# Sixteen experts on one Trainium2 core: smaller rooms by rank, unsplit first layers for seven experts, short last blocks in four column groups

## The chip, the cores and the metric

The kernel runs on one core of a Trainium2 chip. The metric is device microseconds for one execution of the whole program, and the lower number is the better one. Each kernel is one launch; its time is the median of several runs, and beside them stands one execution that the hardware profiler recorded.

## What is computed

Two stages follow one another. The first is a recurrent attention over 4 batches x 8 heads x 768 steps x 40 channels. The second routes its 3072 rows of 320 numbers to 16 experts (4 groups of 4), one expert for each row, and each expert is a two-layer network with 1024 hidden units. The second stage is the one that the change touches:

```python
g_idx = np.argmax(x @ w_group, axis=1)
for g in range(G):
    xg = x[g_idx == g]
    e_idx = np.argmax(xg @ w_expert[g], axis=1)
    for e in range(Eg):
        h = np.maximum(xg[e_idx == e] @ w1[g, e], 0.0)     # 320 -> 1024
        ye = h @ w2[g, e]                                  # 1024 -> 320
        out[tok_idx] = combined[:, None] * ye              # weights of both softmaxes
```

Everything is fp32.

## The kernel before

**Rooms.** The experts are handled one after another in the order of their token counts, the fullest first. The program is fixed before the counts are known, so the expert of rank `r` gets a room of `CAPS[r]` token slots, and all tiles and instructions of rank `r` have that size. With the inputs of this case the reference routes 321, 290, 274, 257, 242, 239, 209, 193, 165, 158, 139, 135, 132, 126, 125 and 67 tokens to the experts by rank. Tokens over a room are left to a loop at the end (`For_i` over `total`, L1048), which takes blocks of 128 tokens, fetches index, rows and both weights anew for each, and runs zero times when every room is large enough. Rank 0 is handled in two parts, `EARLY` and `LATE`.

**One expert** is one call of `expert()`. Its rows `xg` are gathered from DRAM by GpSimd in blocks of 128 (L564), turned on TensorE (`tpm`, three transposes a block) and copied to `xhl`. The first layer makes the hidden units in eight groups `f` of 128 (tile `psh`, three buffers), the ReLU brings them to `hh` (ScalarE the high part L683, VectorE the low part L686; `hh` has one buffer), and the second layer (tile `po`, two buffers) multiplies them with the second weights, a block of up to 128 tokens at a time; the result goes through ScalarE into `y` (L762) and is scattered to the output (L568).

**Precision.** TensorE takes fp32 in two passes, so most operands are split into a high and a low part of a type that takes one pass, and the products that matter are added up. The weights arrive as fp32 in `w1s` (1.5 MB) and `w2s` (1.3 MB), each with two buffers, sent by SyncE's queue; ScalarE rounds them to `w1h`, `w2h` (L624) and VectorE subtracts to get `w1l`, `w2l` (L626). There are three kinds of first layer. A split one has 8 matmuls of W columns for each `f` (L729, 64 rows for an expert, where W is the room). A side-by-side one (`NARROW`) has high and low tokens side by side, two matmuls of W and three of 2W columns for each `f` (40 rows). An unsplit one (`FULL`) has 3 fp32 matmuls for each `f` (L697), each shown as two passes (48 rows), and needs no split of `w1s`. In the second layer a full block has three matmuls for each `f` (L750 to L752, 24 rows). A last block of at most 64 tokens, here called a half block, has its high and low tokens side by side and needs two (L755 and L756, 16 rows); its two halves are then added up by VectorE (L764 to L766).

**Order.** The loop `for r in range(NEARLY, NE)` first issues the loads for rank r+2 (`load_ix`, `load_w1`, `load_w2`, `load_x`) and puts the split of the next expert's weights (`split_tasks(r + 1)`) among the ReLUs of rank r: three pieces of `w1s` before the first layer, the four pieces of `w2s` one behind each ReLU. The turns of rank r+1 follow the first layer of rank r (`then`). SyncE and GpSimd each work through their DMAs in order, so a transfer that waits holds back the ones behind it.

## Time and profile before

| what | value |
|---|---|
| median of 3 runs | 445.42 us |
| lowest and highest of them | 444.24 and 445.44 us |
| the profiled execution | 445.48 us |
| its span, first to last instruction | 443.8 us |
| around the span | 1.7 us |
| TensorE busy, share of the span | 398.2 us, 90% |
| VectorE, ScalarE, GpSimd busy | 280.1, 220.4 and 176.3 us |
| mean granted TensorE clock | 0.881 |
| expert stage | about 190 to 438 us |

The page cuts the span into 40 slices of 11.1 us; a digit is the busy share of a slice in tenths. A second view used below takes stretches of time and gives each engine's busy time in them, for one tile alone: a stretch from an expert's first matmul of a kind to its last is the length of that stage.

### The profile page before, as it was taken

How to read it: one execution, taken by the hardware profiler on the slowest of the kernel's cores; microseconds unless marked ns; L12 is line 12 of the kernel's file. 1: busy time of each engine (PE TensorE's matmuls, PEld its weight loads, DVE VectorE, ACT ScalarE, POOL GpSimd, SP SyncE). 2: the span in 40 equal slices, each digit the busy share in tenths (PEclk: the TensorE clock that was granted, in tenths of full speed). 3: DMA queues.
4: the chain of work that ended last, by engine and by line, in shares of the span. 5: the costliest groups of instructions: out<-in, count | busy, mean ns of one | idle time of the engine just before them, and what ended most of it. 6: DMA issues, size and time to landing. Idle time of an engine off the chain costs nothing.

```text
span 443.8 us, 13468 instructions
## 1 busy us (share of the span) xinstructions
PE 398.2 (90%) x5470; PEld 357.5 (81%) x5470; DVE 280.1 (63%) x712; ACT 220.4 (50%) x570; POOL 176.3 (40%) x213
## 2 busy tenths in 40 slices
PE   6688796887787799699999999999999999999994
PEld 2376565765565588499999999999999999999994
DVE  5466285786656875774964665857675878767420
ACT  1426242634445360533854565756474766766421
POOL 4256355555455724545314134333214516322210
PEclk9659685989788755579999999999999999999998
DMA  8826457788795865248966457576676667544400
GB/s 212 228 78 203 145 150 208 213 236 259 221 273 168 250 187 201 60 97 316 371 226 222 150 202 246 199 266 220 203 285 241 212 202 299 194 146 140 158 16 9
DMA packets 29730, 87.80 MB, mean 198 GB/s; under 512 B 11537, under 2 KB 15577, under 8 KB 26051
## 3 DMA queue, kind: packets, MB, share of 16 engines
q1 hardware_dynamic: 24292, 69.52, 49.4%
q0 software_dynamic: 5152, 16.93, 11.1%
q8 instruction: 43, 0.70, 0.7%
q10 hardware_dynamic: 224, 0.49, 0.4%
q14 instruction: 19, 0.16, 0.1%
HBM read 76.77 MB, written 11.01 MB: 198 GB/s over the span
## 4 chain that ended last, share of the span: by engine, by line
PE 69%; issue 10%; DVE 7%; DMA 5%; POOL 4%; ACT 3%; POOLq 1%; SPq 0%; ACTq 0%
PE psh L729 20%; PE po L750 6%; PE po L751 6%; PE po L752 6%; PE busy L134 4%; PE X L254 4%; PE tpm L291 2%; ACT ab L175 2%; PE X L190 2%; PE po L756 2%; PE po L755 2%; PE tp L291 2%; DMA nt<-in_nat_dram 2%; PE psh L697 1%; PE Y L230 1%
## 5 line engine op out<-in xcount | busy, mean ns | idle before, releaser
L175 ACT ACTIVATE ab<-aw,bcol 128x64 f32<-128x64 f32 x192 | 41.9, 332 | 64.0 <-PE aw L172 62.1
L564 POOL DMA_INDIRECT xg<-x_d,ix x34 | 40.2, 1183 | 81.1 <-PE po L752 29.1
L568 POOL DMA_INDIRECT out_dram<-y,ix x34 | 39.8, 1171 | 78.5 <-ACT y L762 64.5
L750 PE MATMUL po<-w2h,hh 128*128 128x320 f32 (+1 forms) x208 | 65.7, 316 | 0.0
L751 PE MATMUL po<-w2l,hh 128*128 128x320 f32 (+1 forms) x208 | 64.2, 309 | 0.0
L752 PE MATMUL po<-w2h,hh 128*128 128x320 f32 (+1 forms) x208 | 64.2, 309 | 0.0
L626 DVE TENSOR_TENSOR w2l<-w2s,w2h 128x640 fp32r<-128x640 f32 x64 | 50.6, 822 | 20.2 <-ACT w2h L624 20.1
L729 PE MATMUL psh<-xhl,w1h 128*128 128x256 f32 (+4 forms) x352 | 60.3, 293 | 2.6 <-DVE xhl L669 2.0
L729 PEld LDWEIGHTS psh<-xhl,w1h 128*128 128x128 f32 x352 | 51.1, 195 | 3.1 <-DVE xhl L669 2.3
L683 ACT ACTIVATE hh<-psh 128x512 fp32r<-128x512 f32 (+5 forms) x68 | 33.4, 491 | 33.7 <-PE psh L729 24.9
L686 DVE SCALAR_TENSOR_TENSOR hh<-psh,hh 128x256 fp32r<-128x256 f32 (+2 forms) x104 | 39.5, 411 | 16.8 <-ACT hh L683 16.2
L624 ACT CAST w2h<-w2s 128x640 fp32r<-128x640 f32 x64 | 43.1, 728 | 0.0
L750 PEld LDWEIGHTS po<-w2h,hh 128*128 128x128 f32 (+1 forms) x208 | 38.9, 187 | 0.1
L751 PEld LDWEIGHTS po<-w2l,hh 128*128 128x128 f32 (+1 forms) x208 | 38.9, 187 | 0.0
L752 PEld LDWEIGHTS po<-w2h,hh 128*128 128x128 f32 (+1 forms) x208 | 38.8, 187 | 0.0
L626 DVE TENSOR_TENSOR w1l<-w1s,w1h 128x1024 fp32r<-128x1024 f32 x26 | 31.7, 1219 | 11.1 <-ACT w1h L624 7.6
L729 PE MATMUL psh<-xhl,wsk 128*128 128x256 f32 (+4 forms) x176 | 36.9, 292 | 0.0
L729 PE MATMUL psh<-xhl,w1l 128*128 128x256 f32 (+4 forms) x176 | 36.8, 291 | 0.0
L134 PE MATMUL busy<-ones_b 128*128 128x512 bf16 x85 | 34.5, 539 | 2.2 <-DVE sep L900 1.2
L762 ACT ACTIVATE y<-po,xg 128x320 f32<-128x320 f32 (+1 forms) x26 | 13.7, 529 | 45.4 <-PE po L752 43.2
L471 POOL DMA_INDIRECT itab<-tokid,slot x24 | 26.7, 1111 | 22.8 <-DVE slot L402 10.3
L285 POOL TENSOR_TENSOR x<-xn,den 128x320 f32<-128x320 f32 x20 | 15.8, 789 | 45.8 <-DVE xn L280 42.6
(198 smaller groups left out, 866.8 us busy)
## 6 DMA issues: line engine op xcount, KB each, us to landing
w1s<-in_w_dram SPq DMA_DIRECT2D x12, 1536.0 KB, 7.4
w2s<-in_w_dram SPq DMA_DIRECT2D x12, 1280.0 KB, 6.7
nt<-in_nat_dram SPq DMA_DIRECT2D x24, 488.0 KB, 4.6
qk<-in_qkT_dram SPq DMA_DIRECT2D x24, 448.0 KB, 6.2
x_d<-x SPq DMA_DIRECT2D x24, 192.0 KB, 3.0
w1s<-in_w_dram SPq DMA_DIRECT2D x8, 384.0 KB, 4.8
w1s<-in_w_dram POOLq DMA_DIRECT2D x2, 1536.0 KB, 7.5
w2s<-in_w_dram SPq DMA_DIRECT2D x8, 320.0 KB, 5.0
```

Source lines behind the costliest of these rows:

```text
L134: mm(t, ones_b, bc(ones_b.unsqueeze(1), (P, 4, P)), start=True, stop=True)
L175: rt["exp"] = nc.scalar.activation(ab[:, i, :], aw[:, i, :], AF.Exp, bias=bcol[:, u, i:i + 1])
L564: return nc.gpsimd.indirect_dma_start(out=o, out_offset=None, in_=src, in_offset=bass.IndirectOffsetOnAxis(ap=idx, axis=0))
L568: return nc.gpsimd.indirect_dma_start(out=out, out_offset=bass.IndirectOffsetOnAxis(ap=idx, axis=0), in_=y, in_offset=None, bounds_check=N ...
L624: nc.scalar.copy(a, src[:, s])
L626: lows.append(lambda: nc.vector.tensor_tensor(o[rows], src[rows, s], a[rows].bitcast(F32), op=ALU.subtract))
L683: act = nc.scalar.activation(hr, src, AF.Relu)
L686: nc.vector.scalar_tensor_tensor(hh[:, f:f + per, dst], src[:, :, t], 0.0, hr.bitcast(F32)[:, :, t], op0=ALU.max, op1=ALU.subtract)
L729: ins = mm(ps[:, g * W:(g + 1) * W], w[:, s], x, start=(n == 0), stop=(n == len(todo) - 1))
L750: mm(po[0:m], hh[:, f, t], w2h[:, s], start=st0, stop=False)
L751: mm(po[0:m], hh[:, f, t], w2l[:, s], start=False, stop=False)
L752: ins = mm(po[0:m], hh[:, f, tl], w2h[:, s], start=False, stop=sp0)
```

## The change

The rooms are smaller: rank 1 goes from 352 to 304, ranks 2 and 3 from 320 and 288 to 288 and 272, and so on to rank 15 from 128 to 96; the second part of rank 0 goes from 128 to 80. Seven experts (ranks 9 to 15) have unsplit first layers instead of three, and ranks 7 and 8 instead of 11 and 12 have side-by-side ones. In `TAIL` are ranks 2, 3, 9, 10, 11 and 12, whose last block has 32 or 16 tokens. It is computed by a new function `short()`: the low part of its hidden units is not made, the fp32 ReLU `h32` is multiplied with the raw `w2s` in 8 fp32 matmuls (two passes each), and these go in turn to four groups of 32 columns of the array, which write four groups of 32 partitions of `po`. ScalarE copies the first group, VectorE adds the other three and multiplies. For three-block experts the short block is issued before block 1, for two-block ones at the end. Because the short block reads `w2s`, a `TAIL` expert issues `load_w2(r + 2)` behind that block's matmuls (`freed`) instead of at the top of the loop, and the new unsplit experts issue `load_w1(r + 2)` behind their first layer, as the old ones did. A half block may now be narrower than the 64 columns that it uses; GpSimd zeroes the rest.

```diff
--- before.py
+++ after.py
@@ -45,16 +45,19 @@
 
 
 
-NEARLY, NPICK, EARLY, LATE = 1, 2, 256, 128
-CAPS = [EARLY + LATE, 352, 320, 288, 256, 256, 256, 256, 192, 192, 192, 192, 160, 160, 160, 128]
-
-
-NARROW = ((0, 1), (11, 0), (12, 0))
+NEARLY, NPICK, EARLY, LATE = 1, 2, 256, 80
+CAPS = [EARLY + LATE, 304, 288, 272, 256, 240, 224, 208, 176, 160, 144, 144, 144, 128, 128, 96]
+
+
+NARROW = ((0, 1), (7, 0), (8, 0))
 
 RETIRE = ((2, 0), (5, 0), (8, 0), (11, 0), (13, 0), (14, 0))
 
 
-FULL = (13, 14, 15)
+FULL = tuple(range(9, NE))
+
+
+TAIL = tuple(r for r in range(1, NE) if 0 < CAPS[r] % P <= 32)
 
 
 def bc(ap, shape):
@@ -670,18 +673,30 @@
 
         return [lambda i=i, m=m: one(i, m) for i, m in enumerate(blocks(W))]
 
-    def expert(key, W, ws, xg, idx, between=(), then=None, last=None):
+    def expert(key, W, ws, xg, idx, between=(), then=None, last=None, freed=None):
         xhl = xhls[key]
         w1h, w1l, wsk, w2h, w2l = (ws.get(n) for n in ("w1h", "w1l", "wsk", "w2h", "w2l"))
 
         nf = W // P * P if 0 < W % P <= 64 else W
         mp = W - nf
-        hh = pools["hp"].tile([P, NF, 2 * W], F32R, name="hh")
+        tail = key[0] in TAIL
+        mq = 0 if tail else -(-mp // 32) * 32
+        hh = pools["hp"].tile([P, NF, 2 * (nf + mq)], F32R, name="hh")
+        if mq > mp:
+            for a in (W, W + mq):
+                nc.gpsimd.memset(hh[:, :, a:a + mq - mp].bitcast(F32), 0.0)
+        if tail:
+            h32 = pools["hp"].tile([P, NF, mp], F32, name="h32")
 
         def relu(f, per, src):
-            hr = hh[:, f:f + per, 0:W]
-            act = nc.scalar.activation(hr, src, AF.Relu)
-            for dst, t in ((slice(W + mp, 2 * W), slice(0, nf)), (slice(W, W + mp), slice(nf, W))):
+            hr = hh[:, f:f + per, 0:nf if tail else W]
+            act = nc.scalar.activation(hr, src[:, :, 0:nf] if tail else src, AF.Relu)
+            if tail:
+                nc.vector.tensor_scalar(h32[:, f:f + per, :], src[:, :, nf:W], 0.0, None, op0=ALU.max)
+                nc.vector.scalar_tensor_tensor(hh[:, f:f + per, nf:2 * nf], src[:, :, 0:nf], 0.0, hr.bitcast(F32),
+                                               op0=ALU.max, op1=ALU.subtract)
+                return act
+            for dst, t in ((slice(nf + 2 * mq, 2 * (nf + mq)), slice(0, nf)), (slice(nf + mq, W + mq), slice(nf, W))):
                 if t.start < t.stop:
                     nc.vector.scalar_tensor_tensor(hh[:, f:f + per, dst], src[:, :, t], 0.0, hr.bitcast(F32)[:, :, t],
                                                    op0=ALU.max, op1=ALU.subtract)
@@ -736,9 +751,26 @@
         if key in NARROW:
             with tc.issue_after(act.ins):
                 do(between)
-        for i, m in enumerate(blocks(W)):
+        def short(i, m):
+            po = pools["ps_o"].tile([P, DM], F32, name="po")
+            for f in range(NF):
+                g = 32 * (f % 4)
+                mm(po[g:g + m], h32[:, f, :], w2st[key[0]][:, f * DM:(f + 1) * DM], start=(f < 4), stop=(f >= 4))
+            if freed:
+                freed()
+            y = pools["hp"].tile([P, DM], F32, name="y", bufs=3)
+            nc.scalar.copy(y[0:m], po[0:m])
+            for g in range(32, P, 32):
+                nc.vector.tensor_tensor(y[0:m], y[0:m], po[g:g + m], op=ALU.add)
+            nc.vector.tensor_scalar(y[0:m], y[0:m], xg[i][0:m, 3 * P:3 * P + 1], None, op0=ALU.mult)
+            no_order("out", scatter(y[0:m], idx(i, m, 1)))
+
+        nb = blocks(W)
+        for i, m in enumerate(nb[:-1] if tail else nb):
+            if tail and i == 1:
+                short(len(nb) - 1, mp)
             t = slice(i * P, i * P + m)
-            tl = slice(W + mp + i * P, W + mp + i * P + m)
+            tl = slice(nf + 2 * mq + i * P, nf + 2 * mq + i * P + m)
             po = pools["ps_o"].tile([P, DM], F32, name="po")
             for f in range(NF):
                 s = slice(f * DM, (f + 1) * DM)
@@ -753,7 +785,7 @@
                 else:
                     if not st0:
                         mm(po[0:m], hh[:, f, t], w2l[:, s], start=False, stop=False)
-                    mm(po[0:2 * m], hh[:, f, nf:nf + 2 * m], w2h[:, s], start=st0, stop=sp0)
+                    mm(po[0:2 * mq], hh[:, f, nf:nf + 2 * mq], w2h[:, s], start=st0, stop=sp0)
                     if st0:
                         mm(po[0:m], hh[:, f, t], w2l[:, s], start=False, stop=False)
             y = pools["hp"].tile([P, DM], F32, name="y", bufs=3)
@@ -761,11 +793,13 @@
             if m > 64:
                 nc.scalar.activation(y[0:m], po[0:m], AF.Copy, scale=comb)
             else:
-                nc.scalar.copy(y[0:m], po[m:2 * m])
+                nc.scalar.copy(y[0:m], po[mq:mq + m])
                 nc.vector.tensor_tensor(y[0:m], y[0:m], po[0:m], op=ALU.add)
                 nc.vector.tensor_scalar(y[0:m], y[0:m], comb, None, op0=ALU.mult)
             done = scatter(y[0:m], idx(i, m, 1))
             no_order("out", done)
+        if tail and len(nb) == 2:
+            short(1, mp)
         if key in RETIRE:
 
             with tc.issue_after(done.ins):
@@ -1029,7 +1063,8 @@
             load_ix(r + 2)
             if r not in FULL:
                 load_w1(r + 2, nc.gpsimd if r < 2 else None)
-            load_w2(r + 2, nc.gpsimd if r < 2 else None)
+            if r not in TAIL:
+                load_w2(r + 2, nc.gpsimd if r < 2 else None)
             xgs[r + 2] = load_x(CAPS[r + 2], ix_of(r + 2))
         if r + 1 < NE:
             split = split_tasks(r + 1)
@@ -1040,7 +1075,8 @@
             then = []
         if r in FULL and r + 2 < NE:
             then.append(lambda r=r: load_w1(r + 2))
-        expert((r, 0), CAPS[r], wsp_[r], xgs[r], ix_of(r), split, then)
+        freed = (lambda r=r: load_w2(r + 2)) if r in TAIL and r + 2 < NE else None
+        expert((r, 0), CAPS[r], wsp_[r], xgs[r], ix_of(r), split, then, freed=freed)
 
 
     hp = pools["hp"]
```

Three places show how the instructions move. First TensorE at the end of rank 9 (`po` and `hh` are its second layer and hidden units) and the start of rank 10 (`psh`), before:

```order
L755 MATMUL po_5696<-w2l_5403,hh_5562 64x320
L756 MATMUL po_5696<-w2h_5402,hh_5562 128x320
L729 MATMUL psh_5743<-xhl_5653,w1h_5553 128x192 x4
L729 MATMUL psh_5743<-xhl_5653,wsk_5555 128x192 x2
L729 MATMUL psh_5743<-xhl_5653,w1l_5554 128x192 x2
L729 MATMUL psh_5743<-xhl_5653,w1h_5553 128x192 x4
L729 MATMUL psh_5743<-xhl_5653,wsk_5555 128x192 x2
```

and of the changed kernel:

```order
L782 MATMUL po_5605<-w2h_5463,hh_5537 128x320
L783 MATMUL po_5605<-w2l_5464,hh_5537 128x320
L784 MATMUL po_5605<-w2h_5463,hh_5537 128x320
L758 MATMUL po_5635<-w2s_5178,h32_5538 32x320 x8
L712 MATMUL psh_5666<-xhl_5589,w1s_5358 128x144 x6
L712 MATMUL psh_5680<-xhl_5589,w1s_5358 128x144 x6
L712 MATMUL psh_5692<-xhl_5589,w1s_5358 128x144 x6
```

The pairs of the half block are gone: a full block of three matmuls for each `f` is followed by eight short ones of 32 rows, and the first layer of rank 10 is unsplit.

Second SyncE's queue from the first weights of rank 11 to those of rank 12, before:

```order
L582 DMA w1s_5545<-in_w1_dram 128x3072 [waits DMAHW0_49,DVE_49]
L582 ISA
L582 DMA w2s_5547<-in_w2_dram 128x2560 [waits DMAHW7_49,DMAHW1_49,DVE_49]
L574 TENSOR_LOAD ewi_69
L597 ISA
L597 DMA ix_5723<-itab_58 128x2x2 [waits DMASW3_49,DMASW4_49,DMASW2_49,DMASW1_49]
L582 ISA
L582 DMA w1s_5725<-in_w1_dram 128x3072 [waits DMAHW3_49,DVE_49]
```

and of the changed kernel:

```order
L585 DMA w1s_5603<-in_w1_dram 128x3072 [waits DMAHW0_49,PE_49]
L585 ISA
L585 DMA w2s_5644<-in_w2_dram 128x2560 [waits DMAHW1_49,DMAHW7_49,DVE_49,PE_49]
L577 TENSOR_LOAD ewi_69
L600 ISA
L600 DMA ix_5658<-itab_58 128x2x2 [waits DMASW3_49,DMASW2_49,DMASW1_49]
L585 ISA
L585 DMA w1s_5730<-in_w1_dram 128x3072 [waits DMAHW3_49,PE_49]
```

Both loads of weights now wait for TensorE (`PE_49`), `w1s` for the first layer of two ranks earlier and `w2s` for the short block of two ranks earlier; the index load `ix` of rank 12 stands behind both.

Third ScalarE from the copy of rank 9's last block on, through the first layer of rank 10, before (`w2h_5763` is the high part of rank 11's second weights):

```order
L764 COPY y_5713<-po_5696 64x320
L624 CAST w2h_5763<-w2s_5547 128x640 x4
L683 ACTIVATE hh_5742<-psh_5743 128x2x192
L683 ACTIVATE hh_5742<-psh_5767 128x2x192
L683 ACTIVATE hh_5742<-psh_5789 128x2x192
L624 CAST w1h_5913<-w1s_5725 128x1024 x2
L683 ACTIVATE hh_5742<-psh_5811 128x2x192
```

and of the changed kernel (`w2h_5676` is the same):

```order
L762 COPY y_5646<-po_5635 32x320
L693 ACTIVATE hh_5664<-psh_5666 128x2x128
L693 ACTIVATE hh_5664<-psh_5680 128x2x128
L693 ACTIVATE hh_5664<-psh_5692 128x2x128
L627 CAST w2h_5676<-w2s_5644 128x640 x3
L693 ACTIVATE hh_5664<-psh_5704 128x2x128
L627 CAST w2h_5676<-w2s_5644 128x640
```

The pieces of rank 11's `w2s` stood ahead of all ReLUs (`hh`) of rank 10 and now stand ahead of the last of the four only; they wait for a load that is issued later.

## Rows read from the trace of the kernel before

**Rows 1.** Page, slices of the span: TensorE's busy tenths and its granted clock.

```profile
PE   6688796887787799699999999999999999999994
...
PEclk9659685989788755579999999999999999999998
```

**Rows 2.** First layers by stretch (`psh`): length, PE, PEld, DVE, ACT busy (count), clock, DMA.

```profile
205.87:211.04 5.17, 5.04 (x40) 4.69 (x40) 1.54 (x6) 1.70 (x7) 1.00 0.77 203
216.17:226.03 9.86, 9.86 (x61) 9.73 (x61) 3.62 (x7) 3.28 (x7) 1.00 0.97 367
237.45:246.99 9.54, 9.54 (x64) 9.29 (x64) 3.72 (x14) 3.06 (x7) 1.00 0.47 159
257.36:265.92 8.56, 8.56 (x64) 8.48 (x64) 3.50 (x14) 2.90 (x7) 1.00 0.50 167
321.52:329.03 7.51, 7.51 (x64) 7.47 (x64) 2.06 (x3) 1.80 (x3) 1.00 0.82 293
336.72:343.85 7.13, 7.13 (x64) 7.12 (x64) 1.76 (x6) 1.47 (x3) 1.00 0.95 345
377.69:384.22 6.53, 6.49 (x40) 5.71 (x40) 1.92 (x6) 2.05 (x7) 1.00 0.65 221
390.73:396.62 5.89, 5.80 (x40) 5.21 (x40) 1.71 (x6) 1.90 (x7) 1.00 0.67 243
403.12:409.64 6.52, 6.52 (x48) 6.44 (x48) 1.66 (x6) 1.31 (x3) 1.00 0.58 214
428.86:434.14 5.28, 5.28 (x48) 5.28 (x48) 1.27 (x3) 1.16 (x3) 1.00 0.10 33
```

**Rows 3.** Second layers by stretch (tile `po`), the same columns.

```profile
226.93:237.45 10.52, 10.52 (x72) 10.39 (x72) 0.00 (x0) 1.06 (x2) 1.00 0.65 224
397.19:400.80 3.61, 3.61 (x25) 3.60 (x26) 0.00 (x0) 0.00 (x0) 1.00 0.19 56
400.80:403.12 2.32, 2.32 (x18) 1.80 (x15) 0.00 (x0) 0.53 (x1) 1.00 0.20 35
```

**Rows 4.** Turns of two blocks (`tpm`), TensorE alone: length, busy (count), clock, DMA.

```profile
396.62:397.19 0.57, 0.57 (x6) 1.00 0.12 29
```

**Rows 5.** Timeline of TensorE in attention: start, length, line, operation, tiles, shapes, count.

```profile
128.61 0.86 PE L336 MATMUL lg<-xT,wc 128*32 128x128 f32 x24
129.40 0.68 PE L254 MATMUL X<-nt,pt 64*64 64x41 f32 x32
```

**Rows 6.** Timeline of VectorE from a half block's evacuation (rank 12) on.

```profile
403.77 0.48 DVE L765 TENSOR_TENSOR y<-y,po 32x320 f32<-32x320 f32 x1 [1.81 <-ACT y L764]
404.28 0.37 DVE L766 TENSOR_SCALAR y<-y,xg 32x320 f32<-32x320 f32 x1
404.58 1.54 DVE L626 TENSOR_TENSOR w2l<-w2s,w2h 128x640 fp32r<-128x640 f32 x2
```

**Rows 7.** Timeline of ScalarE there: the copy, then pieces of `w2h`.

```profile
403.32 0.42 ACT L764 COPY y<-po 32x320 f32<-32x320 f32 x1 [1.80 <-PE po L756]
403.64 1.97 ACT L624 CAST w2h<-w2s 128x640 fp32r<-128x640 f32 x3
```

**Rows 8.** DMA issues from 349 to 425 us: count, KB, median us to landing.

```profile
w2s<-in_w_dram SPq DMA_DIRECT2D x4, 1280.0 KB, 7.4
...
xg<-x_d,ix POOLq DMA_INDIRECT x7, 6.3
```

**Rows 9.** The load of `w2s` issued at 402.0 us, no other running.

```profile
DMA to landing us min/median/max: 5.9/5.9/5.9
```

**Rows 10.** Loads at 349.8 (`w1s`) and 355.0 us (`w2s`): starts, landings of both.

```profile
L582 SPq DMA_DIRECT2D w1s<-in_w_dram x1: 333/333/333, 349.8 to 349.8; - x1
...
L582 SPq DMA_DIRECT2D w2s<-in_w_dram x1: 333/333/333, 355.0 to 355.0; - x1
...
DMA to landing us min/median/max: 7.4/8.1/8.8
```

**Rows 11.** Three gathers of `xg` issued from 348 to 367 us.

```profile
DMA to landing us min/median/max: 8.7/8.7/9.9
```

## The prediction

> **What bounds the kernel now.** I read the slices of the page first [rows 1]. From the nineteenth slice to the last but one TensorE is busy nine tenths or more in every slice and its granted clock is nine tenths or more of full speed; ahead of that, in the attention that the change leaves alone, both vary. The stretches of the expert stage say the same without rounding: in every first layer TensorE's busy time is the length of the stretch to within 0.13 us, in every second layer it is equal to it, and the clock column reads 1.00, the upper of its two levels (2.4 GHz) [rows 2, 3]. So the expert stage is bound by TensorE alone, no wait ends last in it, and each microsecond of TensorE work that goes shortens the span until something else is late. The first question is thus what the removed and added matmuls cost, the second which load or engine no longer keeps up.
>
> **Smaller split first layers.** Now 352, 320, 288, 256 and 192 columns take 10.34 (9.86 for 61 of 64 rows), 9.54, 8.56, 7.51 and 7.13 us [rows 2]. From 320 to 288 that is 0.031 us a column; from 256 to 192 it is nearly flat, and 7.13/64 = 111 ns a row looks like a floor that the weight loads set (PEld is as busy as PE there). Rank 1 (304) lies midway between 9.54 and 8.56, 9.05: -1.29. Rank 2 (288): 8.56 - 9.54 = -0.98. Rank 3 (272) midway between 8.56 and 7.51, 8.03: -0.53. Rank 4 stays at 256. Ranks 5 and 6 (240, 224) go to the floor, 7.13: -0.38 each, -0.76. Sum **-3.6**.
>
> **Side by side.** 192 and 160 columns take 6.53 and 5.89, 0.02 us a column [rows 2]. Rank 7 (208) gives 6.85 for 7.51: -0.66. Rank 8 (176) gives 6.21 for the 7.13 of 192 split columns: -0.92. The late part of rank 0 falls from 128 to 80; no row goes below 128. By 0.02 us a column it would be -0.96, by a floor of 111 ns a row nothing much (5.17/40 is 129 ns already for 128 and 256 columns); I take -0.35 and keep 0 to -1. Sum **-1.9**.
>
> **Unsplit first layers.** 160 columns take 6.52 and 128 take 5.28 [rows 2], so 144 midway 5.90. Rank 9 (160 for 192 split): 6.52 - 7.13 = -0.61. Rank 10 (144 for 192 split): -1.23. Rank 11 (144 for 192 side by side): -0.63. Rank 12 (144 for 160 side by side): 0. Ranks 13 and 14 (128 for 160): -1.24 each. Rank 15 falls from 128 to 96: its row is 110 ns, the floor of the split rows, so I take 0 and keep -1.3 (in proportion to the columns) as the other end. Sum **-4.95**.
>
> **Second layers.** Full blocks are 10.52/3 = 3.51 us, or 3.61 alone, a half block is 2.32 [rows 3]. Rank 1's third block has 48 tokens for 96, so 16 rows for 24: 2.32 - 3.51 = -1.19. Ranks 13 and 14 lose their second block: -2 x 2.32 = -4.64, and its turn, half of 0.57 [rows 4]: -0.57. Sum **-6.4**.
>
> **Short blocks in column groups.** Six half blocks (ranks 2, 3, 9 to 12) become 16 passes of 320 columns, four of them at a time. The unsplit row of 110 ns for 128 columns gives 275 ns for 320. That four groups run at once is seen in attention: 24 fp32 passes of 128 columns, in groups of 32 columns, start at 128.61 and the next matmul starts at 129.40 [rows 5], 0.79 us where 24 x 0.11 = 2.64 would be needed one by one; six sets of 0.11 are 0.66, and 0.13 is entry and exit. So a short block is 4 x 0.275 + 0.13 = 1.23 us against 2.32: -1.09 each, **-6.5**. If they ran one by one it would be 16 x 0.275 = 4.4.
>
> The cuts add up to -23.4 (-3.6, -1.9, -4.95, -6.4, -6.5).
>
> **What the evacuation costs.** A short block is copied in 0.42 [rows 7], then has three additions of 0.48 and one multiplication of 0.37 [rows 6]: 2.2 us, where now 1.3. I put it at nothing, since `po` has two buffers: the next block uses the other one, and the short block's own comes up again 3.6 us later at the earliest. The four ReLUs of the next first layer come one in 1.5 us and find three `psh` buffers, so they can be a microsecond late as well. The zeroing on GpSimd (ranks 1, 8) lies beside a first layer of over 6 us.
>
> **What the later loads cost.** This is the term with a sign against the change. A load of `w2s` took 5.9 us with nothing beside it and 8.8 (the larger of the two landings) when `w1s` had left 5.2 us before it and gathers ran beside it [rows 9 to 11]; the median of four is 7.4 [rows 8]. In ranks 9, 10 and 11 `w2s` of two ranks on leaves at the end E of the short block. In the next rank ScalarE makes three ReLUs, then waits for that load, makes three pieces of `w2h` (1.97 us [rows 7]) and only then the last ReLU, which VectorE follows with 0.56 of its low part behind its own pieces (0.77 each [rows 6]). So that low part is there at X + 3.7, with X the landing after E. TensorE wants it at the third matmul of `f` = 6 of block 0: 5.90 (first layer) + 0.57 (turn) + 20 x 0.147 = 9.4 after E. The stall is X - 5.7. With X = 7.4, the median, which also lies midway between the two ends, it is 1.7 in each of ranks 10, 11 and 12: 5.1. In rank 3 the load of rank 4's `w2s` leaves after rank 2's short block, with `w1s` long ahead of it; the same count along its longer first layer gives X - 5.6, and X of 6.4 near the clear row gives 0.8. For rank 14 the load leaves about 1.4 us ahead of the end of rank 12's short block, and X - 5.0 with 7.4 - 1.4 gives 1.0 in rank 13. Rank 5's load overwrites a buffer that is free early and leaves before rank 3's short block: nothing. Sum **+6.9**. All loads at 5.9 (and 0.1 to issue) give about +1.3; all at 8.8 give 3 x 3.2 + 3.3 + 2.5 = +15.4. Next in line behind these are the gathers, which in the new order of SyncE's queue have their index load behind `w2s`.
>
> **The sum.** 445.5 (the profiled execution, which equals the median of 445.4) - 23.4 + 6.9 = 429.0: I forecast **429 us**.
>
> **Rivals.**
>
> (a) The loads are hidden: TensorE is shifted by so much that they land in time, or nothing runs beside them. Then 445.5 - 23.4 + 1.3 = 423.4, with no stall 422, and 421 if rank 15's first layer follows its columns. For it: ScalarE and VectorE no longer split `w1s` for four more experts (ranks 9 to 12). Against: `w1s` leaves 5.4 us ahead of `w2s` in ranks 9 to 11, as at 355 us [rows 10].
>
> (b) The loads are all late (+15.4, 437.5), or the gathers too: beside weights they took 8.7 to 9.9 us [rows 11], and in ranks 12 to 14 they now leave after an index load that stands behind `w2s`. One to two us for each of three ranks make it 435 to 443.
>
> (c) The evacuation becomes the bound of the short blocks. Its chain is 2.2 us against 1.23 on TensorE; if the next matmuls waited for it in each of six, it would be 6 x 1.0 more: 435. Against it stands the second `po` buffer. The Trainium skill, "TensorEngine Tiling (Array Packing)", section "PSUM Bottleneck", says that tiling speeds up the matmuls and not the copy out of PSUM, which may then be the bottleneck; no row of before shows a block with four groups to add up, and the two engines that it advises to use together are the ones that this chain uses.
>
> (d) The groups don't overlap in fp32 matmuls of 320 columns that accumulate in one bank: 4.4 us for a block in place of 1.23, six times, 19.0 more, 448; with the waits of (a) it would be 442.5, with something between them no change. Against it speak the 24 passes in 0.79 us [rows 5], which have the same type and the same groups of 32 columns.
>
> (e) The slower side: one room is too small. The reference routes 239 tokens to a room of 240 in rank 5, 158 to 160 in rank 9 and 126 to 128 in rank 13; the spare places are 1 to 29, and the count that decides is made in the kernel from its own logits. If a single token is over in any rank the loop at the end runs once, with nothing beside it: an index gather of up to 6.3, rows and weights 7.4 [rows 8], a first layer of 5.28 [rows 2], 16 passes of 0.275, that is 4.4, and a scatter taken to be as long as a gather, some 25 us: 429 + 25 = 454. It decides from the first token over.
>
> **How the numbers follow.** My forecast (424 to 435 around 429) has a chance of 0.72; (a) 0.10; (b) 0.09; (c) 0.02; (d) 0.03; (e) 0.04. The range reaches down to 422, where the cuts come in full, and up to 437, where all loads take 8.8 us; left out are the last part of (a), the upper half of (b), (d) and (e), 0.02 + 0.05 + 0.07 = 0.14. A measurement of this kernel can tell about 0.3% (1.3 us) from no change. Faster by more than that: 0.72 + 0.10 + 0.09 + 0.02 = 0.93; within it, the better part of (d): 0.02; slower, (e) and the rest of (d): 0.05.
>
> **What would show it.** Right: stretches of about 5.9 us for the first layers of ranks 10 to 12 and 5.3 for ranks 13 and 14; a short block of 1.2 us in which sixteen passes start in four sets; TensorE idle some 1 to 2 us in block 0 of ranks 10, 11 and 12, ended by a ReLU whose engine waited for `w2s`; loads of `w2s` near 7.4 us there; the clock still at 1.00. Wrong: passes of the short block that start 0.28 us apart (d); idle TensorE ahead of a turn, ended by a gather (b); idle time after a short block that VectorE's `y` ends (c); a body of the loop at the end (e); no idle time at all (a). The forecast fails by more than its range if a pass of a short block has a cost that the 128-column matmuls of attention don't show, or if the waits let the granted clock fall to its lower level (1.2 GHz) for a stretch.

## The result, and the profile after

The changed kernel takes 431.13 us in the median of four runs beside 444.83 us before; the ratio is 0.9668, with a 95% interval of 0.9589 to 0.9746. The forecast was 429 us in a range of 422 to 437, and faster. (One of the four runs, 476.3 us at a mean granted clock of 0.694, is a disturbed one; ratios leave out runs over 1.5% above the fastest of their kernel, medians don't, and the profiles of c0, e2, e5 and e6 below are of such longer executions.) The profiled execution is the one of 433.07 us, with a span of 431.4.

The slices of the changed kernel's page, to be read beside [rows 1]: TensorE's busy tenths and its granted clock.

```profile
PE   5769795979688969879999999999999999999794
...
PEclk8668677789775695569999999999999999999898
```

The expert stage is as full as before but for one slice: the third from the end has a 7 for TensorE and an 8 for the clock, where [rows 1] has nines. The attention ahead of it, whose code is the same, ended 3.0 us later in this execution than in the one of before (rank 0's late part starts at 208.9 and 205.9 us). From run to run this start moves by several us (203 to 212 in the profiles below), and the runs' medians move with it. So the kernels are compared below in the stretch **from rank 1's first matmul to the start of the expert stage's last matmul**, which holds nothing of the attention. It is 222.5 us before and 207.1 after: 15.4 less. Its two ends before:

```profile
215.10 0.65 PE L729 MATMUL psh<-xhl,w1h 128*128 128x352 f32 x3
437.60 0.31 PE L752 MATMUL po<-w2h,hh 128*128 128x320 f32 x1
```

and its end after (it starts at 217.87, the second row of the next block):

```profile
424.97 0.31 PE L784 MATMUL po<-w2h,hh 128*96 128x320 f32 x1
```

First layers after, with the columns of [rows 2]: rank 0's late part (80), rank 1 (304), rank 8 (176 side by side), rank 10 (144 unsplit), rank 13 (128) and rank 15 (96).

```profile
208.91:213.36 4.45, 4.45 (x40) 4.45 (x40) 1.41 (x6) 1.47 (x7) 1.00 0.95 345
217.87:226.87 9.00, 9.00 (x64) 8.87 (x64) 3.57 (x14) 2.97 (x7) 1.00 1.00 410
332.03:338.25 6.22, 6.17 (x40) 5.49 (x40) 1.83 (x6) 1.99 (x7) 1.00 0.53 203
356.78:362.76 5.98, 5.98 (x48) 5.93 (x48) 1.64 (x6) 1.15 (x3) 1.00 0.82 272
392.92:398.38 5.46, 5.46 (x48) 5.43 (x48) 1.27 (x3) 1.15 (x3) 1.00 0.95 311
416.27:421.54 5.27, 5.27 (x48) 5.27 (x48) 1.07 (x3) 0.99 (x3) 1.00 0.08 30
```

Each but the first is as computed, to within 0.2 us: 9.05 was forecast for rank 1, 6.21 for rank 8, 5.90 for rank 10, 5.28 for ranks 13 and 15. Rank 0's late part gave 0.72 where I took 0.35. Its forty rows come in eight groups of five; a group took 0.58 us before and takes 0.56 now, so the smaller room gave little there. The rest is that two of the eight groups lost some 0.55 us together to late rows before (in both profiles of that kernel) and none does now; what held those rows is not shown.

A short block (rank 9) in TensorE's timeline, with the matmul ahead of it and the first one of rank 10:

```profile
355.32 0.31 PE L784 MATMUL po<-w2h,hh 128*128 128x320 f32 x1
355.56 1.28 PE L758 MATMUL po<-w2s,h 128*32 128x320 f32 x16
356.78 0.39 PE L712 MATMUL psh<-xhl,w1s 128*128 128x144 f32 x1
```

Sixteen passes take 1.22 us where a half block takes 2.32 [rows 3], and TensorE goes on at once: no wait in the whole expert stage ends with `y`. With that rival (c) is out. The Trainium skill, "TensorEngine Tiling (Array Packing)", section "PSUM Bottleneck", warns that the copy out of PSUM may become the bound; here the 2.5 us of copy, additions and multiplication (356.96 to 359.49 us) lie beside other work, and the trace doesn't bear the warning out for this place.

The waits of TensorE from 355 to 410 us, in which the profile names what ended them (us in total, times, longest):

```profile
PE po L782 <- ACT hh L693: 2.7, 1, 2.7
PE po L784 <- DVE hh L696: 0.5, 1, 0.5
```

And the last of them in stretches (length, TensorE, PEld, VectorE, ScalarE, GpSimd busy with counts, granted clock, DMA share and GB/s), rank 13's second layer and rank 14's first:

```profile
398.62:401.30 2.68, 2.68 (x21) 2.62 (x19) 0.00 (x0) 0.00 (x0) 0.17 (x1) 1.00 1.06 429
401.30:404.20 2.90, 0.21 (x2) 0.00 (x0) 1.53 (x3) 2.29 (x5) 0.97 (x1) 1.00 0.99 421
404.20:408.00 3.80, 3.65 (x15) 3.25 (x16) 1.83 (x4) 2.00 (x5) 0.36 (x2) 0.55 0.41 150
408.00:412.00 4.00, 4.00 (x38) 4.00 (x38) 3.55 (x6) 3.06 (x7) 0.82 (x1) 1.00 0.12 45
```

TensorE stood for 2.7 us; then the granted clock was at its lower level (1.2 GHz) for most of the next 3.8 us, in which the rows of the second layer follow each other 0.27 us apart and not 0.147. From rank 13's second layer to the end of rank 14's first it took 13.8 us where 9.1 would do: 4.7 lost, some 2 of them to the clock. That the clock falls when the array has nothing to do is also what the Trainium skill says, "TensorE: Matmul & The Clock Gate", section "What's actually happening": throttled is the default, and activity lifts it. The trace agrees here (1.00 ahead of the wait, 0.55 behind it); other waits, in the last section, left the clock as it was.

### The profile page after: what moved, and what is told of

It is laid out like the page before. It is cut to its first block, busy times and chain, and to the rows that moved or that the text cites. A ratio compares the mean times of both kernels' runs of the same rounds, so it can differ in the third digit from the quotient of the medians.

```text
span 431.4 us, 13222 instructions
## 1 busy us (share of the span) xinstructions
PE 380.4 (88%) x5360; PEld 333.8 (77%) x5360; DVE 263.6 (61%) x702; ACT 203.1 (47%) x560; POOL 168.2 (39%) x217
## 4 chain that ended last, share of the span: by engine, by line
PE 61%; DMA 12%; DVE 9%; issue 9%; POOL 4%; ACT 3%; POOLq 1%; SPq 0%; ACTq 0%
PE psh L744 13%; PE po L784 5%; PE po L782 5%; PE po L783 5%; PE busy L137 5%; DMA w2s<-in_w_dram 4%; PE X L257 4%; PE X L193 3%; DMA ix<-itab 2%; PE tp L294 2%; PE Y L233 2%; PE tpm L294 2%; ACT ab L178 2%; PE Y L217 2%; DVE w2l L629 2%
## 5 line engine op out<-in xcount | busy, mean ns | idle before, releaser
L782 PE MATMUL po<-w2h,hh 128*128 128x320 f32 (+3 forms) x200 | 63.6, 318 | 2.7 <-ACT hh L693 2.7
L784 PE MATMUL po<-w2h,hh 128*128 128x320 f32 (+3 forms) x200 | 62.7, 313 | 0.7 <-DVE hh L696 0.5
L783 PE MATMUL po<-w2l,hh 128*128 128x320 f32 (+3 forms) x200 | 62.1, 310 | 0.0
L567 POOL DMA_INDIRECT xg<-x_d,ix x32 | 35.3, 1102 | 51.8 <-DMA ix<-itab 29.7
L693 ACT ACTIVATE hh<-psh 128x256 fp32r<-128x256 f32 (+5 forms) x68 | 29.3, 431 | 38.0 <-PE psh L712 19.8
L712 PEld LDWEIGHTS psh<-xhl,w1s 128*128 128x128 f32 x336 | 41.7, 194 | 2.6 <-ACT y L794 2.1
L712 PE MATMUL psh<-xhl,w1s 128*128 128x144 f32 (+3 forms) x336 | 42.8, 288 | 0.1
L744 PE MATMUL psh<-xhl,w1h 128*128 128x256 f32 (+5 forms) x224 | 37.9, 291 | 2.8 <-DVE xhl L672 2.2
L782 PEld LDWEIGHTS po<-w2h,hh 128*128 128x128 f32 (+3 forms) x200 | 36.6, 183 | 4.0 <-ACT hh L693 3.0
L784 PEld LDWEIGHTS po<-w2h,hh 128*128 128x128 f32 (+3 forms) x200 | 36.7, 183 | 1.8 <-DVE hh L696 1.8
L783 PEld LDWEIGHTS po<-w2l,hh 128*128 128x128 f32 (+3 forms) x200 | 36.7, 183 | 0.0
L744 PEld LDWEIGHTS psh<-xhl,w1h 128*128 128x128 f32 x224 | 32.1, 194 | 3.4 <-DVE xhl L672 2.4
L257 PE MATMUL X<-nt,pt 64*64 64x41 f32 x768 | 21.8, 267 | 13.0 <-DVE pt L199 12.0
L257 PEld LDWEIGHTS X<-nt,pt 64*64 64x64 f32 x768 | 18.5, 174 | 16.8 <-DVE pt L199 13.7
```

What stands on the lines that cost most here:

```text
L257: mm(X[halves(b), a, cols_of(2 * r + m, base=4 * L)], t["pt"][halves(a), r, cols_of(k, L)], t["nt"][halves(a), cols_of(4 * r + k)], start= ...
L567: return nc.gpsimd.indirect_dma_start(out=o, out_offset=None, in_=src, in_offset=bass.IndirectOffsetOnAxis(ap=idx, axis=0))
L712: ins = mm(ps[:, g * W:(g + 1) * W], w1s[:, s], xhl[:, k, :], start=(k == 0), stop=(k == 2))
L744: ins = mm(ps[:, g * W:(g + 1) * W], w[:, s], x, start=(n == 0), stop=(n == len(todo) - 1))
L782: mm(po[0:m], hh[:, f, t], w2h[:, s], start=st0, stop=False)
L783: mm(po[0:m], hh[:, f, t], w2l[:, s], start=False, stop=False)
```

## The experiments

Three sets of runs, each on one chip, with the kernel before beside every kernel. "Stretch" is as above. The column of ranks 10 to 14 is from rank 10's first matmul to rank 15's; with no wait at all it would be 52.4 with short blocks, by the lengths of their pieces; with half blocks it is 55.3 where the profile names no wait (e1, e6).

| kernel | set | stretch, us | ranks 10 to 14, us | median, us | ratio to before (95%) |
|---|---|---|---|---|---|
| before, first profile | - | 222.5 | 64.8 | 444.83 | 1 |
| before again (b0) | 2 | 222.5 | 64.8 | 442.78 (one run) | - |
| changed, first profile | - | 207.1 | 59.5 | 431.13 | 0.967 (0.959 to 0.975) |
| changed (c0) | 1 | 207.2 | 59.2 | 437.72 | 0.973 (0.962 to 0.985) |
| changed (c1) | 3 | 204.0 | 56.3 | 427.85 | 0.963 (0.954 to 0.971) |
| e1, half blocks | 1 | 205.5 | 55.3 | 435.44 | 0.972 (0.964 to 0.980) |
| e6, short blocks in ranks 2 and 3 alone | 2 | 204.0 | 55.3 | 425.52 | 0.963 (0.954 to 0.971) |
| e2, split behind the ReLUs | 1 | 203.3 | 55.8 | 432.09 | 0.963 (0.954 to 0.972) |
| e3, `w2s` of rank 15 later | 3 | 205.9 | 58.2 | 432.72 (one run) | - |
| e4, e2 and e3 | 1 | 203.4 | 55.7 | 436.59 | 0.971 (0.961 to 0.981) |
| e5, e4 and the index early | 2 | 200.7 | 53.4 | 424.58 | 0.953 (0.942 to 0.965) |
| e5 again (c2) | 3 | 202.2 | 55.0 | 425.04 | 0.950 (0.939 to 0.962) |
| e7, e5 with one column group | 2 | 218.7 | 62.2 | 442.52 (one run) | - |
| e8, room of 64 for rank 15 | 3 | - | 56.9 | 467.59 (one run) | - |

### The changed kernel and the one before, again

> The changed kernel again, beside the three variants below on one chip, so that they can be compared with it. 428 to 433 us; in the profile waits of 0.5, 0.9, 1.0 and some 4 us in block 0 of ranks 10 to 13, as in its first profile. If the 4 us of rank 13 were an accident of that one execution, they are near 1 here.

Measured: 207.2 in the stretch, 59.2 in ranks 10 to 14; the long wait was there again, this time in rank 12 (2.2 us). In the third set:

> The changed kernel beside e5 on one chip. Some 16 us below the kernel before; from rank 1's first layer to rank 15's second layer 207.1 us as in its two other profiles (before: 222.5).

Measured: 204.0. The waits of that profile from 350 to 411 us, and rank 13's second layer in stretches:

```profile
PE po L784 <- DVE hh L696: 0.9, 2, 0.7
PE po L782 <- ACT hh L693: 0.4, 1, 0.4
PE psh L712 <- ACT xhl L667: 0.3, 1, 0.3
```
```profile
396.26:400.50 4.24, 3.50 (x24) 2.97 (x22) 2.50 (x4) 3.26 (x7) 1.51 (x2) 1.00 1.02 425
400.50:404.00 3.50, 3.50 (x30) 3.50 (x31) 2.11 (x4) 2.47 (x6) 1.01 (x1) 1.00 0.83 348
```

No single wait is longer than 0.7 us, the clock stays at 1.00, and ranks 10 to 14 take 3 us less than in the two other profiles. So the price of the waits is not constant: 7.1, 6.8 and 3.9 us over the 52.4 without them. What differs is when `w2s` lands, shown below.

> The kernel before, for a profile on the same chip as the variants: rank 0's late part took 13.6 to 14.4 us in the last four profiles and 9.0 in the first one of the changed kernel. If that is of the chip and not of the change, it is 4 to 5 us longer than 9.2 here too; if the change brought it, it is 9.2 again. From the start of rank 1's first layer to the start of rank 15's second layer 219 to 222.5 us as before.

Measured: rank 0's late part 9.2, the stretch 222.5. The stretch of the kernel before repeats to 0.1 us, as that of a kernel with no wait should. On the chip of this set the longer late part was seen in no kernel, so the question that the run was for, whether the chip of the first set does it to the kernel before too, stays open.

### What are the short blocks worth?

> TAIL empty: the six last blocks are half blocks of 16 rows again, and all loads of w2s are issued at the top of the loop; rooms and kinds of first layer stay. My theory: each half block costs 2.3 us where the short one takes 1.2, six times +1.1 = +6.6; but the waits of ranks 10 to 13, 6.6 us together, come from the loads that the short blocks hold back, and they go. So the time is that of the changed kernel to within 2 us (about 429). Rival 1, the waits come from the unsplit first layers or the smaller rooms (less TensorE time for the same transfers): they stay, 435 us. Rival 2, the short blocks cost more than their stretch shows: faster than the changed kernel by more than 2 us.

```diff
-TAIL = tuple(r for r in range(1, NE) if 0 < CAPS[r] % P <= 32)
+TAIL = ()
```

Measured: the profile names no wait of TensorE from 350 to 420 us, ranks 10 to 14 take 55.3 us, and the stretch is 205.5: 1.6 less than two of the three profiles of the changed kernel and 1.5 more than the third. My theory holds: the waits come with the loads that the short blocks hold back, and they cost about what the short blocks give. (By the medians alone, 435.44 beside 437.72 for c0, the second rival could not be told from it; the stretch tells.)

> The changed kernel with short blocks in ranks 2 and 3 alone; ranks 9 to 12 have half blocks and early loads of w2s. My theory: ranks 2 and 3 keep their gain (0.9 and 0.8 of e1_half_blocks), ranks 9 to 14 take 68.3 us as in e1; from rank 1 on 203.8, 3.3 less than the changed kernel (207.1) and 1.7 less than e1 (205.5). Rival: the late load of rank 4's weights costs what the short blocks give, and it is that of e1.

```diff
-TAIL = tuple(r for r in range(1, NE) if 0 < CAPS[r] % P <= 32)
+TAIL = tuple(r for r in range(1, NE) if 0 < CAPS[r] % P <= 32 and r < 9)
```

Measured: 204.0, as expected. Ranks 2 and 3 keep their gain, since the load held back there has a block and a first layer of 8 us ahead of it, and no wait of `w2s` shows. So all of the loss comes with the short blocks of ranks 9 to 12: with these four more (3.9 us less for ranks 9 to 12, by e6 and e5 below) the changed kernel is 0 to 3.2 us slower than this one in the stretch.

> As e5_index_early, with all eight matmuls of a short block in one column group, one accumulation and no additions on VectorE. My theory: a short block takes 16 x 0.275 = 4.4 us in place of 1.2, since only the four groups run beside each other; six times 3.2 makes 19 us more than e5, about 219.5 from rank 1 on. Rival: a matmul with 16 or 32 columns of weights is short in any place; then a short block stays near 1.2 us and the time is that of e5.

```diff
-                g = 32 * (f % 4)
+                g = 0
-                mm(po[g:g + m], ..., start=(f < 4), stop=(f >= 4))
+                mm(po[g:g + m], ..., start=(f == 0), stop=(f == NF - 1))
-            for g in range(32, P, 32):
-                nc.vector.tensor_tensor(y[0:m], y[0:m], po[g:g + m], op=ALU.add)
```

Two of its short blocks (ranks 2 and 9), in the columns of [rows 3]:

```profile
248.24:252.66 4.42, 4.42 (x17) 1.68 (x16) 0.00 (x0) 0.53 (x1) 1.00 0.20 52
359.25:363.67 4.42, 4.42 (x17) 1.67 (x16) 0.00 (x0) 0.53 (x1) 1.00 0.42 171
```

Both have 32 tokens; the blocks of 16 tokens (ranks 3 and 10 to 12) take 4.41. Measured: 4.42 us a block, 276 ns a pass, and 18.1 us more than e5 in the stretch (six times 3.2, less 1 us of waits that e5 had). So in 1.22 us the groups do run four at a time, also where they accumulate in one bank; few columns of weights without the groups make nothing faster here. Rival (d) is what would have come without it.

### Where do the waits come from?

The chain of the changed kernel that ends in rank 11's second layer (start, length, what), from the load on:

```profile
368.87 6.46 DMA w2s<-in_w_dram
...
375.36 0.74 ACT w2h L627
...
376.11 2.22 DVE w2l L629 x3
...
378.51 0.34 DVE hh L696
...
378.90 0.42 PE po L784
```

Landing, one piece of `w2h`, three of `w2l`, the last ReLU's low part, then the matmul that waited: the path of the prediction, link by link. The low part is there 3.5 us after the landing (3.7 was forecast).

> The split of the next expert's w2s is issued behind the last ReLU in ranks 10 to 13, in place of among the ReLUs; all loads stay where they are. My theory: TensorE waited because the last ReLU stood behind the pieces of w2h, not because a second layer lacked its weights. The waits of ranks 10, 11 and 12 (0.5, 0.9, 1.0) go to 0, that of rank 13 from 4.3 to about 1, since one piece still stands ahead of the copies of the next turn: about 5.5 us faster than the changed kernel, 424. Rival, the transfers themselves bound this stretch: the wait moves to the next turn or the next second layer and the time stays within 1.5 us of the changed kernel.

```diff
+LATER = (10, 11, 12, 13)
...
-                do(between, 1)
+                if key[0] not in LATER:
+                    do(between, 1)
...
-        if key in NARROW:
+        if key in NARROW or key[0] in LATER:
             with tc.issue_after(act.ins):
                 do(between)
```

```profile
PE tpm L295 <- DMA xg<-x_d,ix: 1.5, 1, 1.5
PE psh L713 <- DVE hh L702: 0.7, 1, 0.7
PE psh L713 <- ACT xhl L668: 0.2, 1, 0.2
```

Measured: no second layer waits any more, and the stretch is 203.3 where c0 beside it had 207.2. That is 3.9 less, not 5.5: a wait of 1.5 us (1.7 in the stage) has come up ahead of a turn in rank 11, ended by a gather of `xg`, and 0.9 us at rank 14's first layer. The rival was right for a part: some of the wait moved on.

> As e2_split_behind_relu, and the load of w2s for rank 15 is issued behind rank 13's first layer in place of right behind the load for rank 14. My theory: the load for rank 14 took 10.2 us because the one for rank 15 ran beside it from 1.5 us on; alone it lands in 6 to 8 us, and what is left of rank 13's wait goes: 1 us less than e2_split_behind_relu, some 6.5 us less than the changed kernel, 423. Rival, it is slow for another reason (index and row gathers beside it): it takes some 10 us again and the time is that of e2_split_behind_relu, or the load for rank 15 comes too late and rank 14 waits.

```diff
-            if r not in TAIL:
+            if r not in TAIL and r != 13:
                 load_w2(r + 2)
...
+            if r == 13:
+                then.append(lambda r=r: load_w2(r + 2))
```

```profile
PE tpm L295 <- DMA xg<-x_d,ix: 2.4, 2, 2.0
```

Measured: 203.4, as e2. Rank 13 no longer waits (9.3 us in place of 9.7 in e2), but ranks 11 and 14 wait for gathers. The second edit alone:

> The changed kernel with one edit: the load of w2s for rank 15 is issued behind rank 13's first layer, no longer 1.5 us behind the one for rank 14. ScalarE's order stays. My theory: the wait of about 4 us in rank 13's second layer was rank 14's load, 10.2 us long because rank 15's ran beside it; alone it takes 6 to 8 us and the wait falls to 1 or 2 us; ranks 12 and 13 together take 21.5 to 22.5 us in place of 24.2 and 24.6. Rival: the load is slow for another reason (rank 14's w1s, sent 4.6 us ahead of it, or the gathers): it takes some 10 us again and ranks 12 and 13 take some 24.

Measured, TensorE's waits from 350 to 416 us:

```profile
PE po L782 <- ACT hh L693: 1.6, 2, 1.2
PE po L784 <- DVE hh L696: 1.3, 2, 0.7
PE psh L712 <- ACT xhl L667: 0.3, 1, 0.3
```

Ranks 12 and 13 take 22.7 us, where the changed kernel took 24.2, 24.6 and 21.9. In the first profile of the changed kernel the load for rank 14, issued at 391.6 us, and ScalarE's wait for it:

```profile
L585 SPq DMA_DIRECT2D w2s<-in_w_dram x1: 333/333/333, 391.6 to 391.6; - x1
...
  ACT w2h L627: 4.3, 1
...
DMA to landing us min/median/max: 10.2/10.2/10.2
```

It took 10.2 us with the load for rank 15 1.5 us behind it. But with that load as close behind it ScalarE could start on it 8.0 us after its issue in c1 and 6.6 in e2; with that load 5 to 7.6 us behind it, it was 6.8 us in e4, 8.9 in e3 and 10.8 in c2, below. So my explanation of the long landing falls: the company of rank 15's load doesn't decide it. What does stays open; landings of the same load vary between executions of one program.

> As e4_both, and the index of each rank's rows is loaded one rank earlier, so that it no longer stands behind the held-back load of w2s in SyncE's queue. My theory: in e2 and e4 the wait of 1.2 to 2 us ahead of a turn (ranks 11 and 14) is a gather that left late because its index landed late; with the index early both go, and ranks 10 to 14 take 52.5 us together (11.4, 11.4, 11.1, 9.2, 9.2) in place of 55.7; from rank 1 on 200.5 us in place of 203.4. Rival: the gather is slow because it runs beside the weights; then it leaves earlier but the waits stay above 1 us each.

```diff
+        for q in ((3, 4) if r == NEARLY else (r + 3,)):
+            if q < NE:
+                load_e(q, ...)
+                load_ix(q)
...
-            load_e(r + 2, ...)
-            load_ix(r + 2)
```

```profile
PE psh L713 <- ACT xhl L668: 0.6, 1, 0.6
```

Beside this `ix` gets a sixth buffer. Measured: 200.7, as expected to 0.2 us; ranks 10, 11 and 12 take 11.45, 11.45 and 11.13 us, and no wait of TensorE ends with a gather. The one wait left, ahead of rank 14's first layer, is for the copies of its turn, which stand on ScalarE behind the first piece of a late `w2s`. That settles what the late gathers waited for: their index. In e2 GpSimd stood still for 2.5 us until it landed and then sent the gather that TensorE waited for; in e5 GpSimd still waits for an index (2.5 and 3.6 us), but about a rank earlier. That traffic had no part is not shown: the awaited gather of e2 landed some 8.7 us after its issue, those of e5 and c2 in ranks 9 to 11 after 3.8 to 6.4 us.

> The kernel of e5_index_early again, beside the changed kernel. My theory: 200.7 us from rank 1 on, 6.4 less than the changed kernel, and as much less in the medians: some 22 us below the kernel before. Rival: the e5 profile was a lucky one; waits of several us at ranks 10 to 14 appear here and the medians are within 3 us of each other.

```profile
PE psh L713 <- ACT xhl L668: 2.2, 1, 2.2
```

Measured: 202.2, 1.8 less than c1 on the same chip, and 425.04 against 427.85 us in the medians; of the ratios to before, 0.950 and 0.963, the intervals overlap. The wait for rank 14's turn was 2.2 us this time. I had expected 6.4 us; what came, 2.8 us between the medians, is within the 3 us of the rival, though with one wait and not several. So e5 beats the changed kernel by 2 to 6 us in the stretch, with an order of instructions alone, and the medians do not tell the two apart; e1 and e6 say that without it the short blocks in ranks 9 to 12 could as well be left out.

### What does a room that is too small cost?

> The changed kernel with a room of 64 in place of 96 for rank 15, which has 67 tokens: three tokens are over, and the loop at the end runs once. My theory: rank 15's first layer stays at 5.28 us (floor of the rows), its second layer falls from 3.6 to 2.3, and the loop's body adds some 25 us behind it: index, rows and weights 3 to 6 and 7, first layer 5.3, second layer 4.4, scatter 3. So some 24 us more than the changed kernel, about 453. Rival 1: weights and rows that are gathered come as fast as other loads and the body costs under 15 us. Rival 2: the gather of weights by rows is slow, over 35 us.

```diff
-CAPS = [..., 128, 128, 96]
+CAPS = [..., 128, 128, 64]
```

Rank 15's first layer, then the body of the loop at the end:

```profile
410.53:415.78 5.25, 5.25 (x50) 5.25 (x49) 0.88 (x3) 1.36 (x4) 0.99 (x1) 1.00 0.08 30
421.00:437.00 16.00, 0.00 (x0) 0.00 (x0) 2.24 (x16) 0.00 (x0) 3.85 (x4) 0.56 0.63 199
437.00:452.00 15.00, 13.90 (x45) 10.47 (x45) 2.31 (x7) 0.00 (x0) 0.00 (x0) 0.50 0.00 0
452.00:466.00 14.00, 8.06 (x23) 5.29 (x22) 1.13 (x3) 0.00 (x0) 1.01 (x1) 0.74 0.01 1
```

Measured: from rank 15's start to the end of the span 55.4 us, where c1 beside it took 15.3: the pass costs 40 us, not 25. Its transfers are done after 16 us, with TensorE idle and the clock falling; then the clock is at 0.50, and the first layer takes 15.1 us in place of 5.3, the second 6.1 in place of 4.4. The clock explains the second layer (its rows are 0.53 us apart at first and 0.27 once the clock is back at 1.00), but it brings the first only to some 10.5: there four rows of 128 partitions and two of 64 take turns, and at each change and right behind it the rows are 0.35 to 0.38 us apart, elsewhere 0.21. The end of the range for rival (e) was 454; it would have been some 470. Rank 15's first layer is 5.25 us with 64 tokens, 5.27 with 96 and 5.28 with 128 [rows 2]: the floor that the prediction took from the split rows is there.

## Why the prediction was right

**The bound.** TensorE bounded the expert stage, and what was taken from it came off. In the stretch and rank 0's late part together 15.7 us went, where 16.5 were forecast. That the medians differ by 13.7 and land 2 us from the forecast is in part chance: the attention ahead moves by several us, and the changed kernel's medians were 437.72 and 427.85 us in the first and the third set, beside 451.25 and 445.21 before.

**The cuts.** Forecast -23.4 in all; the pieces in the profile after give about -22.4.

| term | forecast | in the profile after |
|---|---|---|
| smaller split first layers | -3.6 | -3.4 |
| side by side | -1.9 | -2.4 |
| unsplit | -4.95 | -4.4 |
| second layers | -6.4 | -6.4 |
| short blocks | -6.5 | -5.8 |
| waits | +6.9 | +7.1 (c0 6.8, c1 3.9) |

The unsplit ones fell short by some 0.1 us in each of ranks 10 to 13, and that belongs to the short blocks. Rank 10's first layer in e1, where a half block is ahead of it, has the same rows, with ReLUs and splits beside it, as the 5.98 us above:

```profile
362.66:368.54 5.88, 5.88 (x48) 5.82 (x48) 1.47 (x6) 1.23 (x3) 1.00 0.70 250
```

Ranks 11 and 12 are the same (5.88 for 5.98), rank 13 is 5.36 for 5.46 (forecast 5.28). A short block itself takes 1.20 to 1.22 us, as forecast, but the block ahead of it takes 3.69 in place of 3.61 and what comes behind it 0.1 more, so the change to column groups costs some 0.1 us at each edge; the Trainium skill, "TensorEngine Tiling (Array Packing)", section "Key Properties", says that a change of the tiling mode drains TensorE. The trace fits that, but the same 0.1 also stands behind a wait (rank 14's first layer takes 5.46 in e5, 5.36 in e1), so the mode as its cause is not shown. The 0.13 of the prediction, entry and exit, is within the 1.22; the edges come on top and were put at nothing. A short block is thus worth some 0.95 us and not 1.09 (rank 10 takes 11.45 us in e5 and 12.40 in e1).

**The waits** were the right mechanism with the right sum, but the sum was right by luck. The weak step is the landing time X. For ranks 10 to 12 I took 7.4 from the median of four loads [rows 8]; the chains show 6.2, 6.5 and 6.3 us after the issue, and the stalls were 0.4, 0.8 and 0.9 by the stages in place of 1.7 each. Rank 3 did not wait (0.8 forecast). The path itself holds: with these landings, which are 6.3 to 6.7 behind the end of the short block, X - 5.7 gives 0.6 to 1.0. Rank 13 lost 4.7 us with the beginning of rank 14, in place of 1.0: its load left 1.3 us ahead of the end of the short block and took 10.2 us, for which X - 5.0 gives 3.9, and behind the wait the clock was down, which the prediction had only among what would make it wrong. So three stalls smaller than forecast and one larger came to the forecast sum, and the other two profiles of the changed kernel distribute the waits otherwise. The bounds of +1.3 to +15.4 were worth more than the value between them.

**Side by side.** The late part of rank 0 was put at nothing much under a floor of 111 ns a row, but forty rows of 111 ns make 4.44 us, 0.73 less than the 5.17 before and what was measured. That agreement is luck too: most of the 0.72 is the late rows of before, as said above.

**The rivals.** (a), hidden loads, is what e5 comes near to by moving instructions. (b) has a true core: with e2 the gathers were next in line, through their index, as the prediction said, but it was not the time of the changed kernel. (c) and (d) are out by the timeline and by e7. (e) did not come: in the three profiles of the changed kernel the loop ran zero times, with as little as one place to spare. Had it come, e8 says that it would have cost 40 us and not 25; the parts that the prediction names add up to 29.7 as they stand, and most of the rest is a first layer of 15.1 us for 5.28.

## What to carry to other kernels

A cheaper way of computing that reads its input in raw form keeps that buffer busy for longer, and the next load starts later: before the gain is counted, follow the load to the first instruction that waits for it, and what stands behind that one on its engine. Here the four short blocks of the later ranks were worth nothing in the stretch until the split was moved behind the ReLUs and the index ahead of the held-back load. A wait of TensorE is to be priced by its rows behind it too, since the clock may come back at half.

## What the runs showed that was not expected

**The clock behind a wait.** In ranks 10 to 14 waits of up to 1.5 us left the granted clock at 1.00 (e2, e3). Of those of 2 to 3 us some did (2.2 ahead of rank 14 in c2, 2.0 in e4) and some were followed by a stretch at half clock (2.7 in rank 13 of the first profile, 2.2 in rank 12 of c0), so a wait of that length has two prices. Nor is a short wait always safe: in rank 0's late part the clock was at 0.50 for 6.8 us behind two waits of 0.5 and 0.65 us (e1 and e4, alike) and behind one of 1.4 (e2). This part brought the largest such cost: in the four profiles of the first set it took 13.6 to 14.4 us, in all others 9.0 (9.2 before). The profile of c0, with the columns of the stretches above:

```profile
211.00:213.40 2.40, 2.40 (x23) 2.38 (x22) 0.80 (x3) 1.12 (x4) 1.79 (x3) 1.00 0.82 245
213.40:215.40 2.00, 0.13 (x2) 0.00 (x0) 0.22 (x2) 0.35 (x2) 1.88 (x3) 1.00 0.41 128
216.10:222.90 6.80, 6.80 (x32) 6.63 (x32) 4.43 (x12) 5.16 (x11) 1.48 (x2) 0.50 0.93 369
222.90:226.00 3.10, 3.10 (x23) 3.10 (x22) 1.91 (x2) 0.87 (x2) 0.36 (x2) 1.00 0.78 254
```

For 2 us TensorE, VectorE and ScalarE all stood nearly still, with no transfer that the profile names as what they waited for; then TensorE worked for 6.8 us at half clock, and at 1.00 again behind it. By the length of the late part, 14.3 for 9.0, the wait of some 2 us and the clock behind it cost 5.3 us. The first set's runs of the kernel before are longer too (451.25 us in the median, 444.97 to 455.27), but no profile of it was taken on that chip, and what the engines waited for is not settled.

**Narrow rows.** In a side-by-side first layer the second of two rows of W columns follows the first after 66 ns with 80 columns, and it did after 58 ns with 128 columns before, although in the layers whose rows are all equal nothing goes below 110: over the five rows of a group the mean is 112 ns now. So 110 ns is no floor of the single row, but the mean has not gone below it here.
